# A decode block's forward and backward pass: V loads moved to ScalarE's queue, and weight loads placed one by one

## The chip, the cores and the metric

The kernel runs on one core of a Trainium2 chip. The metric is the time of one execution on the device in microseconds (us). The core has five engines with an instruction stream each: TensorE (PE in the profile; PEld is its weight load), VectorE (DVE), ScalarE (ACT), GpSimd (POOL) and SyncE (SP). SP computes nothing: it issues DMAs. ScalarE and GpSimd can issue DMAs too. An engine takes its instructions in order, so a DMA whose buffer is not free yet holds up all that stands behind it on that engine. All DMAs run on the same 16 DMA engines.

## The reference

One token (x of 640 numbers) goes through a block with adaptive layer norm (scale, shift and gate come from `silu(c) @ w_mod`), attention over a cache, and an MLP mixer; then the gradients of everything but some constants are formed:

```python
mod = silu(c) @ w_mod                       # sa, ca, ga, sb, cb, gb
h = layernorm(x) * (1 + ca) + sa
q = (h @ wq).reshape(32 heads, 192)
p = softmax(q . K / sqrt(192))              # K, V: 32 x 8192 x 192, bf16
x = x + ga * ((p . V) @ wo)
h = layernorm(x) * (1 + cb) + sb
x = x + gb * B(h)                           # a sequence of one: x1 = h, then x1 + gelu(layernorm(x1) @ w3) @ w4
outputs: x, and by jax.vjp dx, dK, dV, dwq, dwo, dw3, dw4, dc, dw_mod
```

K and V are 100.7 MB each; both are read (V twice), and dK and dV, as large, are written.

## The kernel before

**First half (lines 374 to 629).** For each of 32 heads K and V come in tiles of 128 partitions x 32 positions x 192 (1536 KB, half a head). VectorE and TensorE make the scores, ScalarE the softmax weights, TensorE sums that the backward pass will need (`M1`, `M2`), so that K is not read again. Chunks of wq and w_mod (960 KB) and tiles of wo (480 KB, one for two heads) come in between.

**The middle (lines 632 to 1027, and 1046 to 1092).** The end of the forward pass and the gradient of the MLP, a chain of short steps on all engines. Here `wo_l[TL - 1] = load_wo(TL - 1)` (L1066, `load_wo` is L200) is issued by SP, then `load_er(1, ...)` (L367, the transposed softmax weights, 8 KB). `stg0` (L1046) holds the buffer `stg` for rows 5, 6 and 7 to 10 of dw4, which `dw4_act`, `dw4_dve` and `dw4_store` (L960, L948, L952) make and store; rows 0 to 4 are in `dw4s` (part of the buffer `w4b`).

**Second half (lines 1452 to 1545).** 64 steps s, one for each half head, from head 31 down. In step s:

- VectorE sums the dots (`dot_sum`, L347), makes dS4 (L1459) and the product of the next V tile with do (`mul_q(s + 1, 1)`, L1094), which is the last use of V tile s+1; TensorE sums these products (`tree_q`, L1113).
- `dv_groups` makes the dV tile in eight parts, each by TensorE (L1124) and a copy on ScalarE (L1125); `dk_part` (L1129) makes the dK tile on VectorE in two parts.
- GpSimd stores both, `dk_store` (L1414) in mid-step and `dv_store` (L1410) at the end. They use five buffers in turn (`OL`), so that dK or dV of a step waits until the store of five tiles earlier has landed.
- The V tile for step s+5 is loaded into the buffer that tile s+1 had (`v_buf`, four buffers in turn). Before the change, SP issues this load (L1495, by `load_v`, L328) early in the program order of the step.
- At the end of the step ScalarE issues `load_er(s + 2)`, and VectorE begins on V tile s+2 (`mul_q(s + 2, 0)`).

**The plan.** Besides, gradients of the weights are made by generators: `g_do` (transposes a wo tile and forms do of two heads), `g_dwo` (overwrites a wo tile with its gradient and stores it, L1227), `g_ld` (loads a wo tile), `g_dq` and `g_wm` (half or two halves of a 960 KB chunk of wq or w_mod: `g_chunk`, which overwrites the chunk and stores it), `g_dw3`, `g_small`, `g_bcast`. `at(s0, n, g)` places n parts of a generator at step s0 and each quarter of a step after it; `slot()` is called four times a step and runs what is due. So a place such as 44.5 means step 44, third slot. `next_w` (L1146) loads the next chunk on SP, in turn into the buffers `w_st` and `stg`; before the change it is called from within `g_chunk`, after the first half of a chunk, and by the last `g_dw3`. The wo tiles share two buffers (`wo_st`), so that tile n+2 can be loaded only when dwo of tile n has landed; `g_ld(n)` is placed 3.25 steps ahead of `g_do(n)`. Four stores at the end (`dwo` of tiles 1 and 0, and two chunks of dw_mod) are held back by `put` and issued by `g_held` (L1229) at fixed places.

SP's queue thus has V tiles, wo tiles and chunks in the order of the program, and GpSimd's queue has all stores.

Of the kernel before, what the change touches and what calls it, by code (L numbers as in the profile page):

```python
# [9 lines left out]
BF16 = mybir.dt.bfloat16  # L10
# [10 lines left out]
def kernel(  # L21
# [26 lines left out]
    nc = tc.nc  # L48
    P = 128
# [6 lines left out]
    JH = J // 2  # L56
# [143 lines left out]
    def load_wo(t):  # L200

        w = wst.tile([P, 3, D], BF16, name="wo_st", tag="wo")
        nc.sync.dma_start(out=w, in_=wo_v[t])
        return w
# [119 lines left out]
    NVB = 3  # L324
    VB = [vp.tile([P, JH, DH], BF16, name=f"VB{b}") for b in range(NVB)]

    def load_v(h, t, v):
        nc.sync.dma_start(out=v, in_=V_hd[h][:, t * JH : (t + 1) * JH, :])  # L328
        return v

    def dot_mul(src, vec):
# [44 lines left out]
    with tc.tile_pool(name="vs", bufs=3) as vsp, tc.tile_pool(name="ft", bufs=2) as ft, \  # L376
# [161 lines left out]
        with tc.manual_schedule(engines=ORDER):  # L538
# [504 lines left out]
    def do_of(h):  # L1043
        return do_r[:, (TL - h // 2) % NDR, (h % 2) * DH : (h % 2 + 1) * DH]

    stg0 = bst.tile([P, ND * CW], BF16, name="stg")  # L1046
    tp_pool.update(p=psT, t="t")

    def do_mm(t, b=None):
# [13 lines left out]
                scale=rinv[:, h : h + 1],  # L1063
            )

    wo_l[TL - 1] = load_wo(TL - 1)  # L1066
    er_l = {0: er0, 1: load_er(1, nc.sync)}

    def q_bc(h, pool=psB, tag="b"):
# [5 lines left out]

    do_mm(TL, 1)
    dw4_store(dw4s[:, 4 * D : 5 * D], 4, 1)
    dw4_act(stg0, 5, 5, 6)
# [6 lines left out]
    dw4_dve(stg0, 5, 6, 7)  # L1085
    dw4_store(stg0, 5, 2)
    qh = q_bc(H1, psT, "t")
    A_.copy(out=bo[:, 2:ND], in_=h2b[0])

# [52 lines left out]
    cur = {}  # L1142
    held = []
    wseq = []

    def next_w():  # L1146
        if wseq:
            view, n = wseq.pop(0)
            if cur.setdefault("n", 0) % 2 == 0:
# [5 lines left out]
            cur["next"] = w  # L1155

    def g_bcast(src, n, out):
        tp = psS.tile([NF, P], FP32, name="bc_t", tag="s")
# [12 lines left out]
    def g_do(n):  # L1171
        do_t(TL - n, 0)
        yield
        do_t(TL - n, 8)
        yield
        assert done_s[0] >= 4 * (n - NDR + 1)
        do_mm(TL - n)
        done.add(n)
        yield

    def g_ld(n):
        wo_l[TL - n] = load_wo(TL - n)
        yield

    def g_chunk(b, first, v3, rows, dst, n, acc, lay):

        lo = n * CW
        if first:
            cur["w"] = cur.pop("next")
# [24 lines left out]
        V_.tensor_tensor(out=acc, in0=ps, in1=acc, op=ALU.add)  # L1214
        for i in range(ND):
            V_.tensor_scalar(out=stg[:, i, :], in0=v_bc, scalar1=rows[:, i : i + 1], scalar2=None, op0=ALU.mult)
        if first:
            next_w()
        else:
            put(dst[:, :, lo : lo + CW], cur["w"], dst is dwm_v and n < GX)  # L1220
        yield

# [25 lines left out]
    def g_wm(n):  # L1248
        for b in range(2):
            g = 2 * n + b  # L1250
            yield from g_chunk(b, b == 0, dmod[:, 3 * g : 3 * g + 3], sc, dwm_v, n, dsc, PLAIN)

    def g_dwo(n):
        t = TL - n
        w = wo_l.pop(t)
        for k in range(3):
            V_.tensor_scalar(out=w[:, k, :], in0=dao_bc, scalar1=o_col[:, 3 * t + k : 3 * t + k + 1], scalar2=None, op0=ALU.mult)
        put(dwo_v[t], w, t < 2)
        yield

    def g_small():
# [16 lines left out]
        store_vec(x2, out_0[0], "x2")  # L1278
        yield

    def g_dw3(lo, n):
# [4 lines left out]
        if lo == 0:  # L1286
            dw4_dve(o3[:, n * F : n * F + D], 11, 11, 12)
            dw4_store(o3[:, n * F : n * F + D], 11, 1)
        nc.gpsimd.dma_start(out=dw3_v[:, lo : lo + n, :], in_=o3[:, 0 : n * F].rearrange("p (a r) -> p a r", a=n))
        if lo + n == ND:  # L1290
            next_w()
        yield

    def g_finish_x():
        V_.tensor_copy(out=d_sa, in_=dha)
# [21 lines left out]
    def at(s0, n, g):  # L1317
        plan.extend((s0 + 0.25 * k, g) for k in range(n))
# [2 lines left out]
    d = g_do(1)  # L1321
    at(1.25, 2, d)
    at(2.0, 1, d)
    at(2.25, 3, g_bcast(dao, ND, dao_bc))
    at(3.0, 1, g_dwo(0))
    at(4.75, 1, g_ld(2))
    d = g_do(2)
    at(6.0, 1, d)
    at(6.0, 2, d)
    at(6.5, 1, g_dwo(1))  # L1330
    at(6.75, 4, g_bcast(du, NF, du_bc))
    at(7.75, 1, g_dw3(0, 2))
    at(8.0, 1, g_ld(3))
    at(8.25, 2, g_small())
    at(8.75, 1, g_dwo(2))
    at(9.0, 3, g_do(3))
    at(9.75, 1, g_dw3(2, 2))
    at(10.0, 1, g_dwo(3))
    at(10.75, 1, g_ld(4))
    at(11.25, 1, g_dw3(4, 1))  # L1340
    at(13.0, 3, g_do(4))
    at(13.75, 1, g_dwo(4))
    for n in range(5, NT):
        d = DO0 + CWS * (n - 5) if n < NT - 2 else 47.75 + 0.75 * (n - NT + 2)
        at(d - 3.25, 1, g_ld(n))
        at(d, 3, g_do(n))
        at(d + 0.75, 1, g_dwo(n))
    late = list(range(GX, NWM))
    k, t = 0, TL
    while t >= 0 or late:  # L1350
        if t >= 0 and not (late and k % 3 == 2):
            wseq.append((wq_v, t // 2))
            at(CW0 + CWS * k, 5, g_dq(t))
            at(CW0 + CWS * k + 1.25, 5, g_dq(t - 1))
            t -= 2
        else:
            wseq.append((wm_v, late[0]))
            at(CW0 + CWS * k, 10, g_wm(late.pop(0)))
        k += 1
    at(CW0 + CWS * k - 1.0, 2, g_finish_x())  # L1360
    for n in range(GX):
        wseq.append((wm_v, n))
        at(CW0 + CWS * k, 10, g_wm(n))
        k += 1
    at(CW0 + CWS * k - 1.0, 1, g_finish_c())
    for s0 in (60.25, 60.75, 61.25, 62.25):
        at(s0, 1, g_held())
    plan.sort(key=lambda p: p[0])
    NP = len(plan)
# [54 lines left out]
        nc.sync.dma_start(out=v_l[5][:, lo:hi, :], in_=V_hd[h5][:, t5 * JH + lo : t5 * JH + hi, :])  # L1424

    mul_q(0, 0)
    load_v5(0, JQ)
    half_q(0, 0)
    dv_groups(dV0, er, doh, (0, 2, 4, 6))
# [14 lines left out]
    dv_groups(dV0, er, doh, (1, 3, 5, 7))  # L1444
    dv_store(0, dV0, JQ, JH)
    dw4_act(dw4s, 0, 3, 4)
    dw4_act(stg0, 5, 7, 11)
    V_.memset(dha, 0.0)
    V_.memset(dsc, 0.0)
    row = None  # L1450
# [1 line left out]
    for s in range(NS):  # L1452
# [37 lines left out]
        if nxt:  # L1490
            mul_q(s + 1, 1)
            half_q(s + 1, 1)
            v_l.pop(s + 1, None)
        if 0 < s < NS - 5:
            v_l[s + 5] = load_v(*ht(s + 5), v_buf(s + 5))  # L1495
        dv(2)
        tree(0, 4, 8)
        dv(3)
# [15 lines left out]
        if s == 0:  # L1514
            dw4_store(stg0[:, 2 * D : 6 * D], 7, 4)
        if row is not None:
            dq_cols(row)
            row = None
# [57 lines left out]
```

## Time and profile before

| what | us |
|---|---|
| three runs: median (lowest to highest) | 1389.81 (1385.27 to 1391.85) |
| the profiled execution, its own time | 1386.39 |
| its span, first to last instruction | 1384.6 |
| busy: PE, DVE, ACT, POOL | 1154.0, 1109.2, 911.1, 108.6 |
| DMA queue of SP (q1): share of 16 engines, bytes | 60.1%, 342.03 MB |
| DMA queue of GpSimd (q0) | 38.7%, 224.89 MB |
| DMA queue of ScalarE (q10) | 0.1%, 0.51 MB |

The page gives, for 40 equal slices of the span, the busy share of each engine in tenths, the share of the 16 DMA engines and the GB/s that they moved. A table of stretches gives the same for stretches of one's own: start and end in us, length, busy time of each engine with its number of instructions, the granted TensorE clock, the DMA share and GB/s. The order of time of an engine shows its instructions with start, length and, in brackets, the idle time before and what ended it. In lists of waits a row has who waited, for whom, the total in us, how often, and the longest. KB are 1024 bytes, MB are 10^6. When a DMA ended is not in these views; where a text says so, the packets of its queue were counted in order of issue.

### The profile page before, as it was taken

How to read it: one execution, taken by the hardware profiler on the slowest of the kernel's cores; microseconds unless marked ns; L12 is line 12 of the kernel's file. 1: busy time of each engine (PE TensorE's matmuls, PEld its weight loads, DVE VectorE, ACT ScalarE, POOL GpSimd, SP SyncE). 2: the span in 40 equal slices, each digit the busy share in tenths (PEclk: the TensorE clock that was granted, in tenths of full speed). 3: DMA queues.
4: the chain of work that ended last, by engine and by line, in shares of the span. 5: the costliest groups of instructions: out<-in, count | busy, mean ns of one | idle time of the engine just before them, and what ended most of it. 6: DMA issues, size and time to landing. Idle time of an engine off the chain costs nothing.

```text
span 1384.6 us, 30509 instructions
## 1 busy us (share of the span) xinstructions
PE 1154.0 (83%) x12712; PEld 733.4 (53%) x12712; DVE 1109.2 (80%) x1455; ACT 911.1 (66%) x2007; POOL 108.6 (8%) x197
## 2 busy tenths in 40 slices
PE   3898989999998989987867977698778886987974
PEld 2777777777777777633323434343334442533421
DVE  4999999999999999986757677686677866876784
ACT  0777777777777778866545656576556665755754
POOL 0000000000000000111100111011101110110011
PEclk8999999999999999765556556565565555655555
DMA  9999999999999999799999999999999999999989
GB/s 383 396 423 425 424 416 423 413 426 418 424 413 425 415 414 380 252 416 424 422 422 425 426 414 426 426 419 425 426 422 425 417 426 384 419 425 426 422 365 378
DMA packets 76889, 569.38 MB, mean 411 GB/s; under 512 B 7439, under 2 KB 25215, under 8 KB 37199
## 3 DMA queue, kind: packets, MB, share of 16 engines
q1 hardware_dynamic: 51594, 342.03, 60.1%
q0 software_dynamic: 24640, 224.89, 38.7%
q8 instruction: 99, 1.62, 0.4%
q10 hardware_dynamic: 516, 0.51, 0.1%
q14 instruction: 40, 0.32, 0.1%
HBM read 340.97 MB, written 226.44 MB: 410 GB/s over the span
## 4 chain that ended last, share of the span: by engine, by line
issue 44%; DVE 25%; DMA 14%; PE 9%; POOL 5%; ACT 2%; POOLq 0%; SPq 0%; ACTq 0%; DVEq 0%
DVE prod L333 10%; DMA KB<-in_A_k_cache_dram 9%; DVE prod L337 5%; DVE vs L403 4%; DMA out_dram<-qs_bc 3%; PE mp L425 2%; POOL out_dram L1414 2%; POOL out_dram L1410 2%; PE half_ps L343 2%; DMA out_dram<-KB 1%; PE mp L430 1%; POOL out_dram L1227 1%; DVE pq L1094 1%; PE dot_ps L1113 1%; DVE S_h L347 1%
## 5 line engine op out<-in xcount | busy, mean ns | idle before, releaser
L1113 PE MATMUL dot_ps<-pq,ident_bf 128*128 128x256 bf16 x1494 | 365.1, 385 | 27.0 <-DVE dP L347 25.5
L410 ACT ACTIVATE vs<-VB,Ef 128x192 bf16<-128x192 bf16 x840 | 303.6, 447 | 0.0
L1125 ACT CAST KB<-dv_ps 128x768 bf16<-128x768 f32 x312 | 241.4, 805 | 83.5 <-PE dv_ps L1124 82.4
L1113 PEld LDWEIGHTS <-ident_bf 128*128 128x128 bf16 x1494 | 147.1, 121 | 172.8 <-issue 137.1
L333 DVE TENSOR_TENSOR prod<-KB,qs_bc 128x6144 bf16<-128x6144 bf16 x62 | 207.9, 3353 | 24.1 <-DMA KB<-in_A_k_cache_dram 16.6
L1124 PE MATMUL dv_ps<-do_r,er_b 1*128 1x192 bf16 x2016 | 220.9, 327 | 4.3 <-ACT KB L1125 2.8
L1129 DVE TENSOR_TENSOR KB<-qh,dS 128x3072 bf16<-128x3072 bf16 x74 | 128.1, 1753 | 95.3 <-DMA out_dram<-KB 76.4
L425 PE MATMUL mp<-vs,KB 128*128 128x193 bf16 x1984 | 188.6, 246 | 4.5 <-ACT vs L410 2.6
L425 PEld LDWEIGHTS <-KB 128*128 128x128 bf16 x1984 | 168.2, 97 | 13.6 <-DMA KB<-in_A_k_cache_dram 5.3
L904 ACT COPY wT<-wT_ps 128x1024 bf16<-128x1024 bf16 x82 | 79.2, 966 | 106.2 <-PE wT_ps L903 105.8
L1124 PEld LDWEIGHTS <-er_b 1*128 1x128 bf16 x2016 | 68.7, 103 | 141.2 <-issue 138.2
L343 PE MATMUL half_ps<-prod,ident_bf 128*128 128x256 bf16 x744 | 95.1, 279 | 44.0 <-DVE prod L337 43.9
L403 DVE TENSOR_TENSOR vs<-VB,E 128x1728 bf16<-128x1728 bf16 x120 | 123.7, 1052 | 0.3 <-ACT vs L410 0.3
L1094 DVE TENSOR_TENSOR pq<-VB,do_r 128x3072 bf16<-128x3072 bf16 x66 | 115.5, 1750 | 0.0
L337 DVE TENSOR_TENSOR prod<-prod 128x3072 bf16<-128x3072 bf16 x62 | 108.7, 1754 | 1.0
L1094 DVE TENSOR_TENSOR pq<-KB,do_r 128x3072 bf16<-128x3072 bf16 x62 | 108.5, 1750 | 0.0
L343 PEld LDWEIGHTS <-ident_bf 128*128 128x128 bf16 x744 | 72.8, 100 | 62.4 <-issue 53.5
L430 PE MATMUL mp<-vs,KB 128*64 128x193 bf16 x1968 | 105.7, 250 | 0.0
L1125 ACT CAST VB<-dv_ps 128x768 bf16<-128x768 f32 x96 | 74.7, 804 | 39.0 <-PE dv_ps L1124 38.7
L1125 ACT CAST qs_bc<-dv_ps 128x768 bf16<-128x768 f32 x104 | 80.1, 805 | 23.7 <-PE dv_ps L1124 23.2
L390 ACT ACTIVATE E<-S_h,negm 128x256 bf16<-128x256 f32 x31 | 15.7, 508 | 114.5 <-DVE negm L561 112.2
L430 PEld LDWEIGHTS <-KB 128*64 128x64 bf16 x1968 | 78.8, 109 | 19.8 <-issue 19.5
(380 smaller groups left out, 1209.4 us busy)
## 6 DMA issues: line engine op xcount, KB each, us to landing
VB<-in_A_v_cache_dram SPq DMA_DIRECT2D x93, 1536.0 KB
out_dram<-KB POOLq DMA_DIRECT2D x74, 1536.0 KB, 17.2
KB<-in_A_k_cache_dram SPq DMA_DIRECT2D x63, 1536.0 KB
KB<-in_A_v_cache_dram SPq DMA_DIRECT2D x29, 1536.0 KB
out_dram<-qs_bc POOLq DMA_DIRECT2D x25, 1536.0 KB, 17.9
out_dram<-VB POOLq DMA_DIRECT2D x25, 1536.0 KB, 17.7
wo_st<-in_A_wo_dram SPq DMA_DIRECT2D x31, 480.0 KB
w_st<-in_A_wq_dram SPq DMA_DIRECT2D x12, 960.0 KB
```

Source lines behind the costliest of these rows:

```text
L333: V_.tensor_tensor(out=prod, in0=src, in1=vec[:, None, :].to_broadcast([P, JH, DH]), op=ALU.mult)
L337: V_.tensor_tensor(out=prod[:, :, 0:HW], in0=prod[:, :, 0:HW], in1=prod[:, :, DH - HW : DH], op=ALU.add)
L343: T_.matmul(ps, lhsT=ident_bf, rhs=prod[:, :, k : k + TF], start=(k == 0), stop=(k == w - TF))
L403: V_.tensor_tensor(out=vs[:, 0:n, 0:DH].rearrange("p j (a b) -> p j a b", b=4), in0=v[:, v0 : v0 + n, :].rearrange("p j (a b) -> p j a b", ...
L410: A_.activation(out=vs[:, k, 0:DH], in_=v[:, v0 + k, :], func=ACT.Copy, scale=Ef[:, j0 + k : j0 + k + 1])
L425: T_.matmul(mp[:, 0:MW], lhsT=kb[:, j0 + k, 0:P], rhs=vs[:, k, 0:MW], start=(q == 0 and k == 0), stop=(z and k == JQ - 1), skip_group_chec ...
L430: T_.matmul(mp[p0 : p0 + 64, MO : MO + MW], lhsT=kb[:, j0 + k, P:DH], rhs=vs[:, k, 0:MW], start=False, stop=(z and k >= JQ - 2), skip_grou ...
L1094: V_.tensor_tensor(out=pq[:, q], in0=v_l[s][:, q * JQ : (q + 1) * JQ, :], in1=do_of(ht(s)[0])[:, None, :].to_broadcast([P, JQ, DH]), op=AL ...
L1113: T_.matmul(ps[:, q * JQ : (q + 1) * JQ, :], lhsT=ident_bf, rhs=pq[:, q, :, k : k + TS], start=(k == 0), stop=(k == w - TS), skip_group_ch ...
L1124: T_.matmul(ps[:, b, k * DH : (k + 1) * DH], lhsT=er[p0 : p0 + 1, 2 * m + k, :], rhs=doh[p0 : p0 + 1, :], start=True, stop=True)
L1125: A_.copy(out=dV4[:, 2 * q : 2 * q + 2, m * PW : (m + 1) * PW], in_=ps[:, :, 0:PW])
L1129: V_.tensor_tensor(out=dK[:, lo:hi, :].rearrange("p j (a b) -> p j a b", b=4), in0=qh.rearrange("p (a b) -> p a b", b=4)[:, None, :, :].to ...
```

## The change

- V tiles from the seventh on (number 6, loaded in step 1) are issued by ScalarE at the end of the step, behind `load_er(s + 2)`, instead of by SP early in it.
- SP's queue then has only wo tiles and chunks. `next_w` is no longer called within `g_chunk`; a generator `g_nw` of its own is placed 2.75 steps ahead of each chunk. `g_ld(n + 2)` is placed two steps behind `g_dwo(n)`.
- In the middle, SP loads two wo tiles (14 and 13) instead of one, and one chunk of wq. For this, dw4 rows 5 and 6 go to the buffer `wT`, rows 7 to 11 are made by VectorE at places 1.75 and 2.0 (`g_dw4`) into `dw4s`, and dwo of tile 15 is also made in `dw4s`.
- The plan of steps 2 to 14 is written anew (dq of wo tiles 15 and 14 at 5.0 and 6.25 instead of 14.0 and 15.25, and so on), the last chunks have places of their own, and the held stores are at 58.0, 58.0, 58.75 and 60.25 instead of 60.25, 60.75, 61.25 and 62.25.

```diff
-    stg0 = bst.tile([P, ND * CW], BF16, name="stg")
+    dw4t = bst.tile([P, 15 * P], BF16, name="wT", tag="wT")
...
-    wo_l[TL - 1] = load_wo(TL - 1)
+    for t in (TL - 2, TL - 1):
+        wo_l[t] = load_wo(t)
...
-        if first:
-            next_w()
-        else:
+        if not first:
...
-        w = wo_l.pop(t)
+        w = wo_l.pop(t) if n else dw4s[:, 0 : 3 * D].rearrange("p (k a) -> p k a", k=3)
...
+    def g_dw4():
+        dw4_dve(dw4s, 7, 7, 9)
+        yield
+        dw4_dve(dw4s, 7, 9, NF)
+        dw4_store(dw4s, 7, NF - 7)
+        yield
...
     for n in range(5, NT):
-        d = DO0 + CWS * (n - 5) if n < NT - 2 else 47.75 + 0.75 * (n - NT + 2)
-        at(d - 3.25, 1, g_ld(n))
+        d = DO0 + CWS * (n - 5) if n < NT - 3 else (44.0, 47.75, 49.0)[n - NT + 3]
         at(d, 3, g_do(n))
         at(d + 0.75, 1, g_dwo(n))
+        if n + 2 < NT:
+            at(d + 2.75, 1, g_ld(n + 2))
...
+    cw = [CW0 + CWS * i for i in range(10)] + [49.75, 53.0, 56.25]
...
+    at(14.25, 1, g_nw())
+    for c in cw[3:]:
+        at(c - 2.75, 1, g_nw())
...
-    for s0 in (60.25, 60.75, 61.25, 62.25):
+    for s0 in (58.0, 58.0, 58.75, 60.25):
         at(s0, 1, g_held())
...
     mul_q(0, 0)
+    next_w()
     load_v5(0, JQ)
...
-    dw4_act(stg0, 5, 7, 11)
...
-        if 0 < s < NS - 5:
-            v_l[s + 5] = load_v(*ht(s + 5), v_buf(s + 5))
...
         if s + 2 < NS:
             er_l[s + 2] = load_er(s + 2)
+        if 0 < s < NS - 5:
+            v_l[s + 5] = load_v(*ht(s + 5), v_buf(s + 5), nc.scalar)
```

More of the change, by code (lines that the diff above doesn't have):

```diff
@@ L325, with load_v @@
     VB = [vp.tile([P, JH, DH], BF16, name=f"VB{b}") for b in range(NVB)]
-    def load_v(h, t, v):
-        nc.sync.dma_start(out=v, in_=V_hd[h][:, t * JH : (t + 1) * JH, :])
+    def load_v(h, t, v, eng=nc.sync):
+        eng.dma_start(out=v, in_=V_hd[h][:, t * JH : (t + 1) * JH, :])
         return v
@@ L1077 @@
     dw4_store(dw4s[:, 4 * D : 5 * D], 4, 1)
-    dw4_act(stg0, 5, 5, 6)
+    dw4_act(dw4t, 5, 5, 6)
     h2b.append(psS.tile([P, 3], FP32, name="h2_pb", tag="s"))
@@ L1084 @@
     V_.reduce_sum(out=cs, in_=cx, axis=AX.X)
-    dw4_dve(stg0, 5, 6, 7)
-    dw4_store(stg0, 5, 2)
+    dw4_dve(dw4t, 5, 6, 7)
+    dw4_store(dw4t, 5, 2)
     qh = q_bc(H1, psT, "t")
@@ L1141 @@
     GX = -(-2 * ND // 6)
-    cur = {}
+    cur = {"n": 1, "next": []}
     held = []
@@ L1148, in next_w @@
             view, n = wseq.pop(0)
-            if cur.setdefault("n", 0) % 2 == 0:
+            if cur["n"] % 2 == 0:
                 w = wst.tile([P, ND, CW], BF16, name="w_st", tag="w", bufs=1)
@@ L1154, in next_w @@
             nc.sync.dma_start(out=w, in_=view[:, :, n * CW : (n + 1) * CW])
-            cur["next"] = w
+            cur["next"].append(w)
     def g_bcast(src, n, out):
@@ L1188, in g_chunk @@
         if first:
-            cur["w"] = cur.pop("next")
+            cur["w"] = cur["next"].pop(0)
         w = stg = cur["w"][:, :, b * PW : (b + 1) * PW]
@@ L1279, in g_small, with g_nw @@
         yield
+    def g_nw():
+        next_w()
[5 more added lines that the diff above has]
+        dw4_store(dw4s, 7, NF - 7)
+        yield
     def g_dw3(lo, n):
@@ L1285, in g_dw3 @@
             V_.tensor_scalar(out=o3[:, i * F : (i + 1) * F], in0=du_bc, scalar1=n2[:, lo + i : lo + i + 1], scalar2=None, op0=ALU.mult)
-        if lo == 0:
-            dw4_dve(o3[:, n * F : n * F + D], 11, 11, 12)
-            dw4_store(o3[:, n * F : n * F + D], 11, 1)
         nc.gpsimd.dma_start(out=dw3_v[:, lo : lo + n, :], in_=o3[:, 0 : n * F].rearrange("p (a r) -> p a r", a=n))
+        yield
         if lo + n == ND:
             next_w()
-        yield
+            yield
     def g_finish_x():
@@ L1323 @@
     at(2.0, 1, d)
+    at(1.75, 2, g_dw4())
     at(2.25, 3, g_bcast(dao, ND, dao_bc))
[L1325 to L1340, printed above, removed]
+    at(3.25, 3, g_do(2))
+    at(4.0, 2, g_small())
+    at(4.75, 1, g_dwo(0))
+    at(5.0, 5, g_dq(TL))
+    at(6.25, 5, g_dq(TL - 1))
+    at(5.75, 1, g_dwo(1))
+    at(7.5, 4, g_bcast(du, NF, du_bc))
+    at(7.75, 1, g_ld(3))
+    at(7.75, 1, g_dwo(2))
+    at(9.75, 1, g_ld(4))
+    at(9.0, 1, g_dw3(0, 2))
+    at(9.75, 3, g_do(3))
+    at(10.5, 1, g_dw3(2, 2))
+    at(10.5, 1, g_dwo(3))
+    at(12.5, 1, g_ld(5))
+    at(12.0, 2, g_dw3(4, 1))
     at(13.0, 3, g_do(4))
     at(13.75, 1, g_dwo(4))
+    at(15.75, 1, g_ld(6))
     for n in range(5, NT):
-        d = DO0 + CWS * (n - 5) if n < NT - 2 else 47.75 + 0.75 * (n - NT + 2)
-        at(d - 3.25, 1, g_ld(n))
+        d = DO0 + CWS * (n - 5) if n < NT - 3 else (44.0, 47.75, 49.0)[n - NT + 3]
         at(d, 3, g_do(n))
         at(d + 0.75, 1, g_dwo(n))
+        if n + 2 < NT:
+            at(d + 2.75, 1, g_ld(n + 2))
     late = list(range(GX, NWM))
-    k, t = 0, TL
+    k, t = 1, TL - 2
+    wseq.append((wq_v, TL // 2))
+    cw = [CW0 + CWS * i for i in range(10)] + [49.75, 53.0, 56.25]
     while t >= 0 or late:
@@ L1352 @@
             wseq.append((wq_v, t // 2))
-            at(CW0 + CWS * k, 5, g_dq(t))
-            at(CW0 + CWS * k + 1.25, 5, g_dq(t - 1))
+            at(cw[k], 5, g_dq(t))
+            at(cw[k] + 1.25, 5, g_dq(t - 1))
             t -= 2
@@ L1357 @@
             wseq.append((wm_v, late[0]))
-            at(CW0 + CWS * k, 10, g_wm(late.pop(0)))
+            at(cw[k], 10, g_wm(late.pop(0)))
         k += 1
-    at(CW0 + CWS * k - 1.0, 2, g_finish_x())
+    at(14.25, 1, g_nw())
+    for c in cw[3:]:
+        at(c - 2.75, 1, g_nw())
+    at(cw[k] - 0.75, 2, g_finish_x())
     for n in range(GX):
         wseq.append((wm_v, n))
-        at(CW0 + CWS * k, 10, g_wm(n))
+        at(cw[k], 10, g_wm(n))
         k += 1
-    at(CW0 + CWS * k - 1.0, 1, g_finish_c())
-    for s0 in (60.25, 60.75, 61.25, 62.25):
+    at(58.75, 1, g_finish_c())
+    for s0 in (58.0, 58.0, 58.75, 60.25):
         at(s0, 1, g_held())
@@ L1426 @@
     mul_q(0, 0)
+    next_w()
     load_v5(0, JQ)
@@ L1513 @@
         dk_store(s, dK, JQ if s in (0, NS - 1) else 0, JH)
-        if s == 0:
-            dw4_store(stg0[:, 2 * D : 6 * D], 7, 4)
         if row is not None:
```

## The prediction, made before the result was known

> **What bounds the kernel now.** I read the page's second part first, then the DMA queues, then a table of stretches, and only then the waits.
>
> ```profile
> span 1384.6 us, 30509 instructions
> ...
> DMA  9999999999999999799999999999999999999989
> GB/s 383 396 423 425 424 416 423 413 426 418 424 413 425 415 414 380 252 416 424 422 422 425 426 414 426 426 419 425 426 422 425 417 426 384 419 425 426 422 365 378
> ...
> HBM read 340.97 MB, written 226.44 MB: 410 GB/s over the span
> ```
>
> The DMA engines are busy in nearly every slice. At 423 GB/s, the rate of the long steady stretch below, the kernel's 569.38 MB need 1346 us of the 1384.6. So the change, which moves the same bytes, can gain only where those engines idle or crawl. In the table the last two columns are the DMA share (1.0 is full) and GB/s:
>
> ```profile
> 554.00:567.00 13.00, 11.57 (x228) 10.17 (x225) 11.98 (x50) 11.49 (x20) 1.27 (x2) 0.82 0.23 77
> 567.00:583.00 16.00, 14.90 (x131) 9.85 (x127) 15.56 (x16) 13.23 (x20) 4.24 (x7) 0.61 0.99 358
> 583.00:588.00 5.00, 4.47 (x74) 2.97 (x72) 4.94 (x7) 4.88 (x8) 0.53 (x1) 1.00 1.01 360
> 600.00:1150.00 550.00, 443.75 (x3346) 213.03 (x3343) 387.91 (x564) 337.00 (x468) 62.73 (x110) 0.58 1.01 423
> ...
> 1168.00:1178.00 10.00, 2.59 (x24) 1.30 (x23) 9.19 (x22) 2.18 (x3) 1.11 (x2) 0.50 0.83 268
> ...
> 1323.00:1337.00 14.00, 11.69 (x74) 4.21 (x75) 12.94 (x15) 8.36 (x12) 2.34 (x5) 0.50 0.68 285
> ```
>
> There are three holes: the middle (13 us at 0.23, so 10.0 us idle), 1168 to 1178 (1.7 us idle) and 1323 to 1337 (4.5 us idle). From 600 to 1150 nothing is idle. There the compute engines wait for the DMA, not the reverse: VectorE waits for old stores to land before it may overwrite their buffers.
>
> ```profile
> DVE KB L1129 <- DMA out_dram<-KB: 76.4, 20, 8.3
> DVE qs_bc L1129 <- DMA out_dram<-qs_bc: 40.2, 10, 7.7
> ...
> DVE VB L1129 <- DMA out_dram<-VB: 23.3, 6, 8.2
> ```
>
> That is 140 us between 600 and 1320. A microsecond more or less on an engine costs nothing there, as long as stores stay queued.
>
> **The middle.** SP's own order of time shows the first hole:
>
> ```profile
> 554.62 0.59 SPq L367 DMA_DIRECT2D qs_bc<-eT_d  x1
> 559.05 0.34 SPq L203 DMA_DIRECT2D wo_st<-in_A_wo_dram  x1
> 563.11 0.50 SPq L367 DMA_DIRECT2D er_b<-eT_d  x1
> 565.89 2.99 SPq L1424 DMA_DIRECT2D KB<-in_A_v_cache_dram  x2
> 582.08 8.54 SPq L328 DMA_DIRECT2D VB<-in_A_v_cache_dram  x2
> ```
>
> In 12 us SP issues one wo tile (480 KB). The change issues two there, and right behind er_b, at about 563.7, a chunk (960 KB). Both buffers are free by then: the chunk's was held by stg0, which is gone, and tile 15's wo buffer ends with its transposes, since dwo of tile 15 now goes to dw4s. So 480 + 960 KB = 1.47 MB move into idle time. If the DMA stays full afterwards they are worth 1.47 MB / 423 GB/s = **3.5 us**. The chunk pushes the two halves of V tile 5 back by at most those 3.5 us; they are used in step 3 (about 607 us), so nobody waits.
>
> The change also takes work away just behind. Five rows of dw4 (800 KB; four of them stored at 578.54) wait until slots 1.75 and 2.0, near 588 to 592. V tile 6, issued at 582.08, now stands on ScalarE behind er_b of step 1, which was issued at 586.36, and so is about 5 us late. What is left in the queue then ends with the dK half issued at 578.02 (the packets, counted in order of issue, put its end at 582.9), and the chunk pushes that by about 0.5 us. The next store is that of dK of step 1, issued at 585.68 when VectorE has made it; with the 1.6 us that the stores around it take to their first packet, 587.3. So I expect a **new gap** of about 4 us near 583 to 587. The stretch moved 360 GB/s before, so 4 x 360 = 1.44 MB is left for later, 3.4 us. Bounds: 0, if the chunk's push covers it, and 5 us x 360/423 = 4.3. I take 3.4, because VectorE, which sets the next store, is 4.94 of 5 us busy there and cannot be earlier. ScalarE loses four dw4 rows (2.97 us) ahead of it, but waits for TensorE next (1.87 us up to 579.9), so this buys nothing. Middle, net: -0.1 us.
>
> **The V loads on ScalarE.** One more hole, and its cause:
>
> ```profile
> 1145.32 0.33 SPq L328 DMA_DIRECT2D VB<-in_A_v_cache_dram  x1
> 1169.55 0.33 SPq L203 DMA_DIRECT2D wo_st<-in_A_wo_dram  x1
> 1169.97 0.92 SPq L328 DMA_DIRECT2D VB<-in_A_v_cache_dram  x1
> ```
>
> and SP's waits between 1120 and 1200 (total, times, longest):
>
> ```profile
> SPq L203 <- DMA out_dram<-wo_st: 23.8, 1, 23.8
> ```
>
> For 24 us no read is issued: SP waits 23.8 us for a dwo store before a wo load, and the V loads stand behind it. The reads run dry, then the stores, then reads alone crawl at 268 GB/s. In the change only wo tiles and chunks stand behind such a wait, and the last wo load comes 2 steps after the store it waits for instead of in the same slot. I price the hole between 1.7 us (its idle share) and (423 - 268) x 10 = 1.55 MB, 3.7 us, and take **3.2**, nearer to the upper end, because the slow reads come from the same blockage.
>
> What the move costs: a V load may be issued only when its buffer is free, which VectorE does early in the step, and TensorE's sums that ScalarE's last copy stands behind need the same product; so ScalarE never waits for it. Should it wait all the same (the program also has each load wait for the earlier load that used its completion semaphore, two to five steps back, a chunk's among them), the eight dv copies of the next step stand behind it, and the dV store behind those. Issuing takes ScalarE 0.33 us (SP's row) to 0.48 (its own er_b row at 1116.78), 57 times: 19 to 27 us, beside ScalarE's 337 us busy of 550. Hidden; uncovered, 0.5 us a step. The load is issued some 5 us (fast steps) to 9 us (12.5 us steps) later. Tile s+5 is first used at the end of step s+3, three steps or 37 us on, and V loads took 11 to 22 us from issue to their last packet: not late. er_b of step s+2 now queues behind V tile s+4, issued one step earlier; it is needed a step later, so it is late only if a V load takes over about 24 us. None did.
>
> **The end.** From 1324 all loads are done, steps 58 to 60 make stores more slowly than the DMA takes them, and the held stores come only at slots 60.25 to 62.25 (1337 and later): the third hole, 4.5 us. The change issues two held dwo stores at 58.0 (0.98 MB), a chunk's at 58.75, and the last V tile at the end of step 58 instead of early in it (1.57 MB). 1.57 MB alone is 3.7 us, all of it 8.4 us. So the hole closes: **4.5**, bounds 2 (only part of the tile lies in the hole) and 4.6 (by bytes). TensorE and VectorE end at 1367 and the queue at 1382, so up to about 12 us can go before compute sets the end. All other moves of chunks, wo tiles, dw3, dq and dwo lie in steps 3 to 57 under a full DMA queue: 0.
>
> **Sum.** -0.1 - 3.2 - 4.5 = -7.8 us against the profiled execution's own 1386.39 us (span 1384.6 and 1.8 around it): 1378.6. That run lies 3.4 us under the median of the three, so for the median **1382 us**. A measurement of this kernel tells about 0.5% (7 us) from no change; the three runs spread over 6.6 us.
>
> **A rule against it.** The row first: from 600 to 1150 the share is 1.01 with one queue for all reads. The Trainium skill, DMA: Bandwidth & Descriptors, "Rules for kernel authors", says that spreading DMAs over the issuing engines does not help bandwidth, as all run on the same 16 DMA engines. By that the V loads' move would give 0, and the sum would be the middle and the end alone, 1385. I side with the 23.8 us row: what the move removes is a queue's head that waits, not lack of bandwidth.
>
> **Rivals.**
> - *The holes only move* (no change). The reads are later by 5 to 9 us a step, other waits for stores remain, and the end's hole is closed by work that is then missing later. For it: VectorE's 140 us of waits stay, and the middle already nets nothing. Against it: the end has 15 us of queued stores behind compute. Middle -0.1, half of the other two, -3.9: 1386; with none of it, 1390.
> - *The new gap repeats* (slower). In steps 1 to 6 of the second half the queues are not yet deep (stores land 4 to 12 us after issue). If the later V load leaves the DMA empty once in each, every gap costs up to 3.4 us. The gains are 3.5 + 7.7 = 11.2, so from the fourth gap on it is a loss; six give 20.4 - 11.2 = +9, **1399**. Against it: from step 2 on a step of 9 us asks for two stores and a load, 4.7 MB, 11 us of DMA.
> - *The change does not do what it says.* If SP reached the chunk only after the V halves, the middle would lose 3.4 with no gain of 2.3; the program's order puts it before them. Folded into the first rival.
>
> **Chances.** Forecast 0.52, holes move 0.34, gap repeats 0.14. Around the forecast the bounds give -3.5 - 3.7 - 4.6 = -11.8 (no gap, both holes in full) to 0.8 - 1.7 - 2 = -2.9, so a median of 1378 to 1387, which a measured median may miss by 3. With the first rival's 1390 the range is 1374 to 1393. Faster by over 0.5% 0.46, within 0.41, slower 0.13.
>
> **What would show it.** SP: two wo loads near 559 to 562 and a chunk near 564 ahead of the halves of tile 5. A share well under 1 for about 4 us near 583 to 588, and none later. No stretch under 0.95 between 600 and 1310, though SP still waits for dwo stores. A share of 0.95 or more in steps 58 to 60. TensorE waiting for er_b, or ScalarE held at a V load, would be a miss of the costs; a second gap in steps 2 to 6, or a full last stretch without a shorter span, would break the forecast.

## The result, and the profile after

The changed kernel takes 1398.18 us (median of 7 runs, 1393.69 to 1398.88), the kernel before beside it 1389.64 us (7 runs, 1384.65 to 1392.78). The ratio is 1.0054, 95% interval 1.0034 to 1.0074: 0.5% slower, where 0.6% faster (1382 us) was forecast. The profiled execution took 1394.66 us.

The page's second part, of the changed kernel:

```profile
span 1392.9 us, 30457 instructions
...
DMA  9999999999999999799999999999999999999998
GB/s 381 399 423 426 423 423 420 411 427 413 427 415 409 415 416 351 285 416 414 419 425 426 382 426 421 417 416 424 417 412 420 406 424 406 415 411 421 407 405 353
```

The DMA is as busy as before, but more slices lie under 420 GB/s, and one at 382. The table of stretches (last two columns: DMA share, GB/s) says where:

```profile
554.00:567.00 13.00, 11.56 (x224) 9.95 (x221) 11.97 (x47) 11.65 (x20) 1.27 (x2) 0.82 0.43 131
583.00:588.00 5.00, 4.35 (x72) 2.94 (x72) 4.94 (x9) 4.63 (x6) 0.53 (x1) 1.00 0.35 147
600.00:1150.00 550.00, 452.70 (x3287) 214.54 (x3285) 382.13 (x561) 328.97 (x458) 61.37 (x107) 0.55 1.01 417
1168.00:1178.00 10.00, 9.25 (x71) 3.83 (x68) 7.71 (x18) 5.56 (x8) 1.11 (x2) 0.50 1.01 421
1323.00:1337.00 14.00, 11.83 (x88) 5.18 (x86) 11.26 (x21) 8.44 (x12) 2.54 (x4) 0.50 1.01 425
1350.00:1380.00 30.00, 21.05 (x139) 7.37 (x138) 25.93 (x21) 20.26 (x28) 4.24 (x8) 0.50 0.85 360
```

The middle is better filled (0.23 to 0.43), the new gap at 583 is there (0.35), both late holes are closed. But the long steady stretch fell from 423 to 417 GB/s at a full share: 550 x (1 - 417/423) = 7.8 us. From 1190 to 1310 it is 411 in place of 424, 3.7 us more, and a new hole opens behind 1350, where the kernel before had a share of 1.01 and 419 GB/s. The middle, in SyncE's order of time:

```profile
556.25 2.91 SPq L203 DMA_DIRECT2D wo_st<-in_A_wo_dram  x2
562.89 0.50 SPq L367 DMA_DIRECT2D er_b<-eT_d  x1
563.45 0.44 SPq L1155 DMA_DIRECT2D stg<-in_A_wq_dram  x1
565.68 2.99 SPq L1440 DMA_DIRECT2D KB<-in_A_v_cache_dram  x2
```

That is as forecast: two wo tiles, then a chunk 0.6 us behind er_b, ahead of the halves of V tile 5. What the forecast had ruled out is in ScalarE's order of time:

```profile
774.34 0.50 ACTq L367 DMA_DIRECT2D er_b<-eT_d  x1
774.94 0.40 ACTq L328 DMA_DIRECT2D KB<-in_A_v_cache_dram  x1
775.43 0.32 ACT L1074 CAST qh<-q_ps 128x192 bf16<-128x192 f32 x1 [15.03 <-DMA er_b<-eT_d]
```

ScalarE stood 15 us at one er_b load. The program's waits name what it stood for: the completion semaphore that SyncE's chunk load of 734.48 had used before, which reached its count at about 774.3. (Two shorter waits of this kind, 4.0 and 5.9 us, end at 751.80 and 1210.21.) At 784 to 792 a hole of 8 us at 0.87 and 270 GB/s follows.

### The profile page after: what moved, and what is told of

Read it like the earlier page. It is cut to its first block, busy times and chain, and to the rows that moved or that the text cites. A ratio compares the mean times of both kernels' runs of the same rounds, so it can differ in the third digit from the quotient of the medians.

```text
span 1392.9 us, 30457 instructions
## 1 busy us (share of the span) xinstructions
PE 1177.9 (85%) x12712; PEld 740.6 (53%) x12712; DVE 1110.1 (80%) x1459; ACT 907.5 (65%) x2003; POOL 108.8 (8%) x196
## 4 chain that ended last, share of the span: by engine, by line
issue 45%; DVE 26%; DMA 13%; PE 8%; POOL 6%; ACT 1%; POOLq 0%; SPq 0%; DVEq 0%; ACTq 0%
DVE prod L333 11%; DMA KB<-in_A_k_cache_dram 9%; DVE prod L337 5%; DVE vs L403 4%; DMA out_dram<-VB 3%; POOL out_dram L1430 2%; POOL out_dram L1426 2%; PE mp L425 2%; DMA out_dram<-KB 2%; PE half_ps L343 2%; POOL out_dram L1226 1%; PE mp L430 1%; DVE pq L1095 1%; DVE S_h L347 1%; ACT KB L1126 1%
## 5 line engine op out<-in xcount | busy, mean ns | idle before, releaser
L1114 PE MATMUL dot_ps<-pq,ident_bf 128*128 128x256 bf16 x1494 | 377.0, 395 | 42.6 <-DVE dP L347 41.5
L1125 PE MATMUL dv_ps<-do_r,er_b 1*128 1x192 bf16 x2016 | 226.9, 335 | 25.0 <-ACT qs_bc L1126 12.1
```

Source lines behind the costliest of these rows:

```text
L1114: T_.matmul(ps[:, q * JQ : (q + 1) * JQ, :], lhsT=ident_bf, rhs=pq[:, q, :, k : k + TS], start=(k == 0), stop=(k == w - TS), skip_group_ch ...
L1125: T_.matmul(ps[:, b, k * DH : (k + 1) * DH], lhsT=er[p0 : p0 + 1, 2 * m + k, :], rhs=doh[p0 : p0 + 1, :], start=True, stop=True)
```

## The experiments

All ratios are to runs of the kernel before on the same chip, in the same group of runs (its medians there: 1388.5 to 1391.2). Line numbers are those of the kernel that was edited. "Lag" is the time from the end of VectorE's last product of the old tile, which frees a V buffer, to the issue of the V load into it: the mean of some 55 loads between 600 and 1310. It is 0.2 us before and 9.2 after.

**Which part costs: the V loads, or all the rest.**

```
e1 (on the changed kernel)
-        if 0 < s < NS - 5:                              # end of the step
-            v_l[s + 5] = load_v(..., nc.scalar)
+        if 0 < s < NS - 5:                              # behind mul_q(s + 1, 1)
+            v_l[s + 5] = load_v(...)
e2 (on the kernel before): the same move the other way round
```

> The changed kernel with the V loads back on SyncE's queue and at their old place, early in the step, behind mul_q of the next step; all else of the change stays. Theory 1 (late V loads: on ScalarE a V load is issued at the end of the step, behind VectorE's wait for a store's buffer, so reads run dry just while stores drain): the steady stretch from 600 to 1150 goes back from 417 to about 423 GB/s, some 11 us of the loss go, and the median is about 1387, 1384 to 1391, with perhaps the 1168 hole back at up to 2 us. Theory 2 (the new places of wo tiles, chunks and dw3 do the harm, not the V loads): the stretch stays at about 417 and the median at 1395 to 1400.

> The kernel before with one edit: V loads from tile 6 on are issued by ScalarE at the end of the step, behind er_b. Theory 1 (late V loads): the steady stretch falls from 423 to about 417 GB/s and the time rises by 8 to 11 us, less up to 3 for the hole at 1168, which goes: 1395 to 1400. Theory 2 (places of wo tiles and chunks): the stretch stays at 423, the hole at 1168 goes, 1386 to 1390.

e1: 1388.14 us, ratio 0.9988 (0.9972 to 1.0003). e2: 1402.53 us, 1.0093 (1.0068 to 1.0118). So theory 1 holds in both directions: the move of the V loads costs 0.66% in the one plan (1.0054 against 0.9988) and 0.93% in the other; all the rest of the change is worth 0.1%, which is not told from nothing. e2 lies above the 1395 to 1400 that were expected of it. In detail another expectation missed. The stretches of e1:

```profile
600.00:1150.00 550.00, 456.46 (x3312) 215.86 (x3311) 388.64 (x568) 334.11 (x462) 62.94 (x111) 0.55 1.01 418
...
1190.00:1310.00 120.00, 103.17 (x801) 50.38 (x800) 88.69 (x133) 78.00 (x109) 12.60 (x22) 0.59 1.01 423
```

The second came back to 423, the first stayed at 418: one profile of a stretch is no measure of its price.

**The place in the step, and the queue.** e3, e12 and e14 keep ScalarE's queue and put the load behind the second dv group, behind the fifth, and behind the second group of the next step. e11 changes one word: SyncE issues, at the place of the change.

```
e3   + v_l[s + 5] = load_v(..., nc.scalar)     behind mul_q(s + 1, 1)
e12  + v_l[s + 5] = load_v(..., nc.scalar)     behind dv(4)
e14  + v_l[s + 4] = load_v(..., nc.scalar)     behind dv(1), 1 < s < NS - 4
e11  - load_v(..., nc.scalar)  + load_v(...)   at the end of the step
```

> The changed kernel with the V loads still on ScalarE's queue, but early in the step (behind the copies of the first two dv groups and ahead of the third) in place of its end. If theory 1 holds by the place alone, the stretch 600 to 1150 comes back to 421 to 424 GB/s and the median to 1386 to 1391. If it is the third queue itself (loads on ScalarE's queue share the DMA engines worse whatever their place), it stays at 1394 to 1400. If ScalarE is held there by the product of VectorE that frees the buffer, ScalarE shows waits at the load and the gain is half: about 1393.

> The changed kernel with the V loads on ScalarE behind the fifth dv group, about half way between the early place (1391.4 when run) and the end of the step (1398.2). If each microsecond of lateness costs about the same: 1393 to 1396. If only a load behind VectorE's wait for a store's buffer is harmed: as one of the two, 1391 or 1398.

> The changed kernel with the V load on ScalarE still later: behind the second dv group of the next step, some 4 us after the end of the step. Measured so far: 7.5 us ahead of er_b 1391.4, 3.9 ahead 1390.6, 0.6 behind 1398.2. If lateness costs, and more the later: 1403 or more. If the end of the step is harmful for another reason (what stands next to the load there), and a load in the middle of the copies is not: 1391 to 1396.

> The changed kernel with one word changed: the V load stands at the end of the step, as changed, but is issued by SyncE. SyncE does nothing else there, so it waits at the load for its buffer and issues it when VectorE frees it, early in the step, whatever the place. Theory 1 (the time of issue is what counts): as with the V loads on SyncE at the early place, 1387 to 1390, and V is issued some 7 us ahead of er_b. Rival (the order of wo tiles, chunks and V in the program is what counts, not the time): as the changed kernel, 1395 to 1400.

| kernel | queue, place | lag, us | median, us | ratio (95%) |
|---|---|---|---|---|
| e11 | SyncE, end | 0.1 | 1389.22 | 1.0003 (0.9984 to 1.0022) |
| e3 | ScalarE, early | 0.4 | 1391.44 | 1.0010 (0.9995 to 1.0026) |
| e12 | ScalarE, half way | 3.7 | 1390.57 | 1.0017 (0.9999 to 1.0036) |
| changed | ScalarE, end | 9.2 | 1398.18 | 1.0054 (1.0034 to 1.0074) |
| e14 | ScalarE, next step | 10.5 | 1396.59 | 1.0054 (1.0034 to 1.0073) |

e3 misses its 1386 to 1391 by 0.4 us, and its stretch from 600 to 1150 stays at 418 GB/s, where 421 to 424 was expected; e12 came out as the early place does, and not between the two. e11 shows that a place in the program is not a time: SyncE has nothing else to do, runs ahead and issues the load the moment the buffer is free. ScalarE issues it when it gets there. In this plan the time follows the lag, not by the microsecond but with a step between 4 and 9 us; e14 turned out later by only 1.3 us than the changed kernel, so it adds little of a dose, and the 1403 or more expected of it did not come. Nor is it the time of issuing: directly behind er_b the load's issue takes ScalarE 0.95 us in the mean (the forecast had 0.33 to 0.48), in e14 0.35 us, at the same ratio of 1.0054. A late load from another engine than ScalarE was run only in e13, whose time was disturbed (below).

**The semaphore's wait, by itself.** e16 is e12, and e17 the changed kernel, with one slot moved, so that the chunk's load is asked for when its buffer is nearly free.

```
-    at(14.25, 1, g_nw())
+    at(16.25, 1, g_nw())
```

> The changed kernel with V loads on ScalarE half way in the step (1390.6 when run) and the chunk load of slot 14.25 moved to 16.25. In the former ScalarE stood 17.8 us at an er_b whose semaphore that chunk's load had used, and a hole of 6.6 us at 779 to 789 follows. If that wait makes the hole and the hole is lost time: the wait is gone or under 5 us and the median is 1384 to 1387. If the hole only moves: the wait is gone and the time stays at 1389 to 1392. If another load takes its place: a wait of over 10 us is still there and nothing is told.

> The changed kernel with one edit: the chunk load of slot 14.25 at 16.25. V loads stay on ScalarE at the end of the step. At the half-way place this edit took ScalarE's 17.8 us wait out and gave 2.1 us. If the wait is most of the loss: 1389 to 1392. If the late place is: 1394 to 1397, with the small losses from 1000 to 1310 still there. If another long wait of ScalarE for a DMA appears in its place: nothing is told.

ScalarE's waits for a DMA and the stretch 700 to 800, first of e12, then of e16:

```profile
ACT qh L1074 <- DMA stg<-in_w_mod_dram: 17.8, 1, 17.8
```
```profile
700.00:800.00 100.00, 67.76 (x413) 28.89 (x412) 57.80 (x59) 46.84 (x65) 9.63 (x18) 0.50 0.95 394
```
```profile
ACT VB L1126 <- DMA w_st<-in_A_wq_dram: 3.1, 1, 3.1
```
```profile
700.00:800.00 100.00, 78.45 (x500) 34.03 (x499) 63.75 (x66) 54.08 (x75) 9.03 (x17) 0.50 1.01 423
```

The long wait is gone (3.1 us at most; 4.2 in e17), and the stretch is at 423. With e12 and the changed kernel this makes a table of two by two:

| median, us (ratio) | with the wait | without |
|---|---|---|
| load at the end of the step | 1398.18 (1.0054) | e17: 1396.21 (1.0039) |
| load half way | e12: 1390.57 (1.0017) | e16: 1388.46 (0.9996) |

By the ratios the place is worth 0.37% and 0.43%, 5 to 6 us; the wait 0.15% and 0.21%, 2 to 3 us. Each comes out alike both times. The place clears the intervals in the second column and all but clears them in the first; the wait alone, with intervals of 0.15 to 0.2% to each side, does not. Between 700 and 800 e12's profile loses 6.9 us against 423 GB/s; by the medians about a third of that was lost time, and e16 came out between what was expected if the hole is all lost time (1384 to 1387) and if it only moves (1389 to 1392).

e18 puts the load half way in the kernel before:

> The kernel before with V loads on ScalarE behind the fifth dv group (half way), in place of the end of the step (which gave 1402.5, 0.93% over before). If the place in the step is the cause in this base too: 1389 to 1394. If ScalarE's queue or its waits are: 1398 to 1403.

1396.73 us, 1.0047 (1.0030 to 1.0065), lag 3.6: half of e2's 0.93% goes, but 1389 to 1394 is missed. ScalarE has a wait of 15.1 us for a chunk's load there too, and its profile loses 8.5 us against 423 GB/s between 700 and 800. What is left of 0.47% was not taken apart; so the step between 4 and 9 us of lag is not shown for this plan.

**Two runs that were disturbed.** e13 makes SyncE's load late by putting it behind er_b, e15 makes it early by loading each tile in two halves.

```
e13 (changed kernel)  er_l[s + 2] = load_er(s + 2, nc.sync)
                      v_l[s + 5] = load_v(*ht(s + 5), v_buf(s + 5))
e15 (kernel before)   half 0 of tile s + 6 behind mul_q(s + 2, 0), half 1 of tile s + 5 behind mul_q(s + 1, 1)
```

> The changed kernel with both er_b and the V load behind it issued by SyncE at the end of the step. er_b waits for TensorE's last dv product of the step, so the V load behind it on the same queue is issued as late as in the changed kernel, but nothing is on ScalarE's queue and ScalarE is never held. If the time of issue is what costs: 1396 to 1402, as the changed kernel (1398.2). If the third queue or ScalarE's waits cost: 1387 to 1391, as with the V loads on SyncE.

> The kernel before with each V tile from 6 on loaded in two halves: the first as soon as VectorE has used the first half of the buffer (at the end of the step before), the second at the old place. It is the opposite of the change: reads are issued some 5 us earlier. If each microsecond counts in this direction too: 3 to 6 us faster, 1384 to 1387. If the reads of before are early enough already (no loss from 600 to 1150 in its profile, 423 GB/s): within 2 us of before, 1388 to 1392; packets are 6 KB in place of 12.

e13: 1396.95 us, 1.0062 (1.0036 to 1.0087), as the late time would have it; but now er_b stands behind V tiles, and TensorE waits for it:

```profile
PE dv_ps L1125 <- DMA er_b<-eT_d: 67.4, 13, 14.4
```

e15: 1402.70 us, 1.0109 (1.0076 to 1.0142): much slower, where the same or faster was expected. SyncE's and ScalarE's waits show why it says nothing on earliness:

```profile
SPq L1429 <- DMA VB<-in_A_v_cache_dram: 80.1, 18, 15.3
SPq L1429 <- DMA KB<-in_A_v_cache_dram: 74.1, 16, 8.1
```
```profile
ACT qh L1073 <- DMA VB<-in_A_v_cache_dram: 28.1, 2, 18.5
```

With twice as many loads a completion semaphore comes round in half the time, and loads wait for loads.

**The other loads on GpSimd's queue**, once with V on ScalarE as changed (e9), once with V on SyncE as in e1 (e10): `load_wo` in `g_ld` and `next_w` issue by `nc.gpsimd`, but for the chunk in the middle.

> The changed kernel with V loads on ScalarE at the end of the step as changed, but wo tiles and chunks of the second half on GpSimd's queue, among the stores, in place of SyncE's. In the changed kernel a chunk (packets of 1.5 KB) alone in SyncE's queue took 34 to 41 us from its first packet to its last, beside V tiles (packets of 12 KB) in 9 us on ScalarE's queue; before, both in one queue, it took 10 to 12. Theory 1a (the loss at 784 to 792 is ScalarE's 13.9 us wait for such a starved chunk, by a shared completion semaphore): no wait of ScalarE for a DMA over 2 us, no loss between 700 and 800, 3 to 4 us faster than 1398, about 1394.5; the rest of the loss (late V loads) stays. Theory 1b (all is lateness of the V loads): 1397 to 1399. If GpSimd's stores now wait behind loads whose buffers are not free: slower than 1399, and GpSimd shows waits of a load for out_dram.

> The changed kernel with V loads on SyncE, early in the step (1388.1 when run), and wo tiles and chunks of the second half on GpSimd's queue. In the former SyncE still waited 57 us at wo loads and 17 at chunks, and the V loads behind them left holes at 896 to 912 (2.6 us) and 1176 to 1183 (2.7 us). If a blocked head of the queue makes these holes, and GpSimd reaches the loads only when their buffers are free: both go, no stretch from 600 to 1345 loses over 1 us, and the median is 1382 to 1384. If GpSimd is held at them, the stores behind them are late: 1390 or more.

e9: 1406.83 us, 1.0114 (1.0087 to 1.0140), although ScalarE waits for no DMA over 0.4 us; GpSimd now stands 131 us at wo loads and 61 at chunks, ahead of stores. e10: 1394.29 us, 1.0027 (1.0008 to 1.0046); SyncE's waits at these loads are gone, GpSimd is held only 7 us at them, the holes at 896 and 1176 are gone, but the 1382 to 1384 expected of that did not come: it is 0.4% slower than e1, at a lag of 0.03 us. Why is open: lateness of the V loads is not all that can cost 5 us here.

**What the holes were worth.** One run for each gain that the forecast had added up, and one for SyncE's waits.

```
e4 (changed kernel)  held stores back to (60.25, 60.75, 61.25, 62.25)
e5 (kernel before)   held stores at (58.0, 58.0, 58.75, 60.25)
e6 (e1)              load_wo(TL - 2) and the middle's next_w() behind load_v5(JQ, JH)
e8 (e5)              g_do(n), g_dwo(n) of n = 13 and 15 at 44.0 and 49.0, g_ld(15) at 46.75
e7 (e1)              g_ld at d + 3.5 for d + 2.75, g_nw at c - 2.25 for c - 2.75, last do at 49.5
```

> The changed kernel with the held stores back at slots 60.25, 60.75, 61.25 and 62.25. Theory of the tail (bytes used earlier are missing later, compute of steps 60 to 63 makes stores more slowly than the DMA takes them): the three gaps behind 1350 (4.6 us) go and the hole before 1345 comes back at up to 4.5 us, so the median stays within 2 us of the changed kernel's, 1396 to 1400. Rival (the early held stores cost the tail more than they give): about 3 us faster, 1394 to 1396. The forecast's step (the early held stores gain 4.5): 1402 to 1403.

> The kernel before with one edit: held stores at slots 58, 58, 58.75 and 60.25. The forecast's step (the end's hole closes and nothing is late behind it): 4.5 us faster, about 1386 beside 1390.5 of before. Theory of the tail (the bytes are missing behind 1350, where steps 60 to 63 make stores more slowly than the DMA takes them): the idle time of 1323 to 1337 moves to 1350 to 1380 and the gain is 0 to 1.5 us, 1389 to 1391.

> The changed kernel with V loads back on SyncE (1388.1 us when run), and of the middle's two added loads (wo tile 14 and the first chunk) each moved behind the halves of V tile 5. It prices the middle alone. The forecast's step (1.47 MB in idle time is worth 3.5 us): 3 to 4 us slower than 1388.1. Rival (the hole only moves, since the new gap near 583 eats what it gives): within 1 us of 1388.1; in the trace the loss between 540 and 600 would then stay near 15.5 us at 423 GB/s.

> The kernel before with held stores at 58, 58, 58.75 and 60.25 and the last wo load 1.5 steps later, at 46.75 (its buffer's store one step earlier, with do and dwo of tiles 13 and 15 at 44.0 and 49.0), so that SyncE no longer stands 23.8 us at it. The forecast's step for the hole at 1168 (3.2 us for it, by whatever means it goes): 1387, 3 us under the 1390.4 that the held stores alone gave. Rival (the holes only move): 1389 to 1391, and the loss shows up behind 1190 or 1345.

> The changed kernel with V loads on SyncE, early (1388.1 when run), and wo tiles 0.75 steps and chunks 0.5 steps later than changed, so that the stores they wait for have landed. SyncE waited 57 us at wo loads and 17 at chunks there, with holes at 896 and 1176. If these waits are the steady stretch's loss (8.9 us at 423 GB/s from 600 to 1310, 3.2 before): SyncE's waits at wo loads fall under 25 us, the holes go, and the median is 1383 to 1386. If the wo tiles and chunks are now late for their users: 1388 or more, with waits of TensorE or VectorE for them.

| kernel | median, us | ratio (95%) |
|---|---|---|
| e4 | 1396.17 | 1.0043 (1.0026 to 1.0060), changed kernel 1.0054 |
| e5 | 1390.44 | 0.9999 (0.9984 to 1.0015) |
| e6 | 1388.60 | 0.9984 (0.9970 to 0.9998), e1 0.9988 |
| e8 | 1390.93 | 1.0023 (0.9998 to 1.0049) |
| e7 | 1390.95 | 1.0010 (0.9989 to 1.0032), e1 0.9988 |

Nothing gains. e5 closes the hole and another one opens behind it:

```profile
1323.00:1337.00 14.00, 10.34 (x63) 3.61 (x61) 12.93 (x21) 7.28 (x10) 2.46 (x4) 0.50 1.00 412
...
1350.00:1380.00 30.00, 16.99 (x113) 6.01 (x111) 18.86 (x16) 16.79 (x23) 3.19 (x6) 0.50 0.96 405
```

e8 closes the hole at 1168 too:

```profile
1168.00:1178.00 10.00, 6.39 (x54) 2.70 (x52) 1.10 (x1) 5.20 (x7) 0.00 (x0) 0.50 1.00 421
```

Look at the third busy column, VectorE: 1.10 of 10 us, where before, in the hole, it was 9.19. While the DMA idled, compute caught up; now the DMA is full and VectorE waits. In e6 the stretch 583 to 588 runs at 437 GB/s in place of e1's 339: the loads that were put behind fill there what they left empty ahead. e7 cut SyncE's waits at wo loads from 57.3 to 19.5 us, the hole at 896 went, that at 1176 fell to 0.6 us, and it is not faster than e1.

No version is faster than the kernel before by what can be measured well: e1 and e6 come out at 0.9988 and 0.9984, and only e6's interval ends below 1, by 0.0002.

## Why the prediction was wrong

- **What bounds the kernel**: read rightly in part. The DMA is full, but the sum treated each idle microsecond of it as a microsecond of time. In a loop where VectorE waits for stores (140 us of waits) and the DMA waits for VectorE, a hole at one side is mostly the other side's catching up. That is the step behind all three gains, and e5, e6 and e8 measured none of them, within 0.15 to 0.25%. The rival "the holes only move" was right here. The forecast's own sign came too: a full last stretch (1.01 from 1323 to 1337) without a shorter span.
- **The middle**: the order and the new gap came as forecast (0.35 from 583 to 588). The two loads' 3.5 us measured 0 (e6 beside e1, both with early V loads). The gap had two causes in the forecast, dw4's later stores and V tile 6; with the tile back early (e1) the share there is 0.93, so the tile is most of it, and it belongs to the V loads. The forecast had priced this gap (3.4 us), but set it off against the gain that did not come.
- **The V loads**: the failed step. "ScalarE never waits for it", "not late", so hidden: 0, and -3.2 for the hole. The forecast even had the lateness right, 5 to 9 us a step (9.2 measured), and it is true that no engine ever waits for a V tile. But a load that is issued 9 us after its buffer is free can leave the read side short of work, and this happens just where VectorE waits for stores. Around 1000 us of the changed kernel, VectorE:

```profile
990.92 1.75 DVE L1095 TENSOR_TENSOR pq<-VB,do_r 128x3072 bf16<-128x3072 bf16 x1
999.64 1.76 DVE L1130 TENSOR_TENSOR qs_bc<-qh,dS 128x3072 bf16<-128x3072 bf16 x1 [6.97 <-DMA out_dram<-qs_bc]
```

TensorE and ScalarE, which wait in turn for what VectorE makes behind it, and ScalarE's queue:

```profile
1001.64 0.26 PE L1206 MATMUL bc_ps<-vrow,ident_bf 3*128 3x128 bf16 x1 [6.42 <-DVE vrow L1202]
1002.20 0.48 ACT L1208 CAST v_bc<-bc_ps 128x384 bf16<-128x384 f32 x1 [6.03 <-PE dv_ps L1125]
```
```profile
1007.01 1.29 ACTq L328 DMA_DIRECT2D VB<-in_A_v_cache_dram  x1
```

  The buffer was free at 992.7; the load came 14.3 us later, the tile before it had landed at 1000, so from 1000 to 1008 no V packet moved, and from 1008 to 1015 the DMA moved 373 GB/s at a share of 1.02. Five such episodes, at 1008, 1104, 1155, 1249 and 1299, lose 1 to 1.4 us each (in 8 us); with the load half way and no wait (e16) there are ten from 600 to 1310 of 0.6 to 1.1.

  The late place is worth 5 to 6 us (e16, e17); by which of these losses is shown in part only. It is clearest at the start, in the gap near 583 and just behind it, first e17, then e16:

```profile
583.00:600.00 17.00, 13.97 (x169) 8.43 (x169) 16.70 (x28) 15.11 (x24) 3.04 (x5) 0.93 0.77 279
```
```profile
583.00:600.00 17.00, 14.16 (x159) 8.22 (x156) 16.69 (x28) 13.82 (x23) 3.04 (x5) 0.87 0.94 363
```

  Against 423 GB/s that is 5.8 and 2.4 us. In this stretch all seven kernels with a late load (a lag of 8.5 us or more: the changed one, e2, e4, e9, e13, e14, e17) moved 276 to 308 GB/s, the three half way 361 to 377, all with early loads 383 or more. e13 (280 GB/s) loads from SyncE, and TensorE does not wait for er_b there yet: here it is the lateness, whatever the queue. From 600 to 1310 single profiles do not tell them apart: 416 GB/s in the changed kernel and 413 in e17, but also 416 in e3 and 417 in e11, whose loads are early and whose time is that of before. So the episodes behind 600 are seen, and their price is argued.

  The hole at 1168 closed, as forecast, and the 3.2 us for it were not gained (e8).
- **The semaphore**: named in the forecast, priced at nothing. A long wait came once, 15 us, worth 2 to 3 us by the medians (e16, e17), within the noise of each pair.
- **The end**: the hole closed, as forecast, and gained 0 (e5). The step that failed here is "up to about 12 us can go before compute sets the end", from 15 us of stores queued behind compute. Those 15 us are the last two steps' own output, issued from 1362 on: 6.3 MB, 14.9 us at 423 GB/s. As far as three profiles show, what sets the end is when the last step computes, and from 1324 on the steps take their own time. TensorE's last product ends at 1367.1 before, 1369.8 in e5, 1379.3 after.
- **The rule against it**: by the Trainium skill, DMA: Bandwidth & Descriptors, "Rules for kernel authors", spreading loads over issuing engines brings no bandwidth. The runs agree: with the load half way and without the long wait, ScalarE's queue gives 0.9996 (e16). The 0 that was drawn from it for the move was wrong all the same, since the move also made the loads late. The same table of the Trainium skill says, for overlap with compute, to issue a DMA early; the two-by-two table puts a price on it here, 5 to 6 us.
- **A near hit by luck**: the rival "the new gap repeats" had 1399, and 1398.18 was measured. But the gap did not repeat in steps 2 to 6: the changed kernel's share is 0.99 from 588 to 600 and 1.01 from 600 to 700.

What stays open: how the lateness behind 600 turns into time, why the cost sets in between 4 and 9 us of lag in the changed plan, what is left in e18, and why e10 is slower than e1. That earlier loads than before would gain was not shown (e15 was disturbed by its own semaphores).

## What to carry to other kernels

A load that nobody waits for can still have a price, if it is issued late: look for the time at which its buffer is free, and give it to an engine that has nothing else to do, since a place in the program is a time only on an engine that works. Where compute and DMA wait for each other by turns, an idle microsecond of the DMA is not a microsecond of the kernel: ask what the other side did in it. At the end, subtract the last steps' own output before calling the queue a reserve.

## What the runs showed of the hardware

- **Small packets beside large ones.** From 993 to 998 of the changed kernel, three queues had work: 79 packets of 1.5 KB of a chunk (and 7 of a wo tile) began on SyncE's, 82 of 12 KB of V tiles on ScalarE's, and 77 of 12 KB of stores on GpSimd's. So the queues take turns by packets, not by bytes, and SyncE's got 30 GB/s beside 202 and 189. The Trainium skill, DMA: Bandwidth & Descriptors, "Queues, rings and completion order", says that an engine goes round its queues packet by packet, and the trace agrees, as far as its packets are those that the skill means. A chunk of 960 KB took 26 to 31 us from its first packet to its last in the changed kernel, and 16 to 27 before, where it shared SyncE's queue with V tiles (told by the packets' size; the 34 to 41 and 10 to 12 us that stand ahead of e9 do not come out of it). It costs nothing by itself here: in e16 chunks took 24 to 30 us, at 0.9996.
- **Loads alone are not slow.** In the first half of the kernel before, from 60 to 510 us, SyncE's loads moved 187.68 MB and the stores 0.45 MB:

```profile
60.00:510.00 450.00, 413.07 (x6366) 347.80 (x6365) 428.92 (x426) 338.75 (x1104) 8.22 (x15) 1.00 1.01 420
```

  420 GB/s at a full share. So the 268 GB/s of the hole at 1168, where by the forecast "reads alone crawl" and for which it priced the hole above its idle time, is not the rate of loads alone; what made it is open.
- **Completion semaphores are shared** by SyncE's and ScalarE's loads in turn: one load that is long on its way can hold an engine that has nothing to do with it, for a long wait of 14 to 18 us once in each of seven kernels (the changed one, e2, e3, e4, e12, e14, e18), each time for a chunk's load.
